# Forty step durations in a kernel's own order model, set to other values (attention and gated MLP on one core)

## The chip, the cores and the metric

The kernel runs on one core of a Trainium2 chip. The metric is the device time of one execution in microseconds, from three runs of each kernel; beside them stands one profiled execution, with its trace.

## The reference

Eight batches, eight heads, 576 positions, head size 64. Each head has two attentions whose results are added; the result then goes, token by token (4608 tokens of 512), through a gated two-layer product.

```python
q_d = q.reshape(B, H, Sd, 4, D).mean(axis=3)       # k_d and v_d likewise, Sd = 144
out_d = softmax_attention(q_d, k_d, v_d)           # all 144 x 144
out_up = np.repeat(out_d, 4, axis=2)
mask = np.abs(pos[:, None] - pos[None, :]) < 4     # a band of 7 around the diagonal
out_local = softmax_attention(q, k, v, mask)
x = (out_up + out_local)                           # -> 4608 x 512
h = x @ w_in                                       # 512 -> 2048
g = h * np.clip(h + 3.0, 0.0, 6.0) / 6.0
out = g @ w_out                                    # 2048 -> 512
```

## The kernel before, in words

*Work.* The tokens are cut into nine chunks of 512 (n = 0 to 8). For a chunk, x is split into a high and a low part (the lines L875 and the casts through L122 and L120). Then come 16 blocks f. A block of the first product, called gemm1 (L972), is 12 matmuls of 128x128 by 128x512: four depths kk of 128 times three pairs of high and low parts. Its result goes into one of two PSUM banks, h0 and h1. ScalarE takes relu (L978), VectorE the gate (L982, after which the bank is free), ScalarE the high part (L986), VectorE or GpSimd the low part (L990). The second product, gemm2 (L1022), adds three matmuls for each of four quarters m of the 512 tokens into four banks o0 to o3 over all 16 blocks. For f = 0 and f = 15 each quarter is a step of its own; for the blocks between, the four quarters are one step of 12 matmuls. After f = 15 each quarter is evicted (L920 on ScalarE, L922 on VectorE) into one of two buffers of the kind `ob`, and stored in four or five pieces (L926, SyncE's queue). A buffer is free when its store has landed.

*Attention* comes in units (b, hp): batch b, pair of heads hp = 0 to 3. The units of b = 0 and 1 run in single steps before and between the first blocks: rows of q, k turned on TensorE (L318) or VectorE (L301), the sums of four rows of v (L409 on TensorE, L394 on VectorE, L396 and L397 on GpSimd), scores of the averaged part (L446), of the band (L640, L648), transposes (L539, L673), products with v (L620, L691), and the adds into x (L696). The units of b = 2 to 7 run as *bursts*: one step on TensorE in which a new unit's averaged scores (L463) and banded scores (L648) and an older unit's products with v (L691, L608) stand together. A burst takes both gemm1 banks, h0 and h1. They are freed by ScalarE's mean (L623) and four pulls (L120), by VectorE's `mean_too` (L626), and by the two adds (L696). L394 sums v, L346 averages q or k; both stand near the adds in VectorE's queue.

*Order.* The order of all work is made on the host, before the program is built, by a list scheduler inside the kernel (`Plan.emit`). Each step is an `op` with an engine, a duration, what it follows, which buffers it takes, and a due time. `emit` runs its own clock: whenever an engine is free in this clock, it starts there the ready step with the earliest `late` time, which is worked back from due times and durations. The steps are then issued in that order, and on the chip each engine runs its queue strictly in order. For steps that several engines can do, `COST[what]` gives a pair (a, b) per engine and the duration is a + b x size; `PEN` adds to the due time. Which `ob` buffer or PSUM bank a step gets is set by the same clock: the one that came free first there. Two lines carry this:

```python
    return {e: (a + b * size, PEN[what].get(e, 0.0)) for e, (a, b) in COST[what].items()}
    l.sort(key=lambda x: (x[0] - (STAY if e == "PE" and kind and x[2].kind == kind else 0.0), x[1]))
```

So a duration in this table changes no instruction; it changes when `emit` believes an engine or buffer to be free, and with that the order of the queues, the choice of engine for steps with a choice, and the choice of buffers.

## Time and profile before

| what | value |
|---|---|
| median of 3 runs (lowest, highest) | 921.95 us (921.82, 923.52) |
| the profiled execution, its span | 922.62 us, 920.8 us |
| mean granted TensorE clock | 0.996 |
| busy: TensorE, VectorE, ScalarE, GpSimd | 902.3, 535.9, 436.8, 217.6 us |
| gemm2 (L1022), 1728 matmuls; gemm1 (L972), 1728 | 412.2 us; 407.0 us |

The span is the time from the first to the last instruction. Busy time counts computing instructions alone. In a row of a timeline stand start, duration, engine, line and operation, and in brackets the engine's idle time ahead of it with what ended it.

### The profile page before, as it was taken

The numbers are of one execution on the slowest core, as the hardware profiler recorded it, in microseconds if no ns is written. First come the engines' busy times: TensorE is split into PE (matmuls) and PEld (weight loads), VectorE is DVE, ScalarE is ACT, GpSimd is POOL, SyncE is SP. The second block draws the span as 40 slices with busy tenths as digits, with TensorE's granted clock in tenths as the row PEclk, the third lists the DMA queues.
The fourth block names the chain that finished last, engine by engine and source line by source line (L and its number), as shares of the span: only waits on it lengthen the run. The fifth ranks groups of instructions, "written<-read, shape, count | busy, mean of one in ns | idle before, by whom it ended". The sixth has DMA issues, their size and how long they took to land.

```text
span 920.8 us, 19166 instructions
## 1 busy us (share of the span) xinstructions
PE 902.3 (98%) x7013; PEld 734.4 (80%) x7013; DVE 535.9 (58%) x973; ACT 436.8 (47%) x1442; POOL 217.6 (24%) x295
## 2 busy tenths in 40 slices
PE   7899999999999999999999999999999999999997
PEld 4577777888778888888888888888888888888886
DVE  6898875677675557556745585557654432233222
ACT  4698754745654456345645555445542222222221
POOL 4626512133342233123302250223201000000000
PEclk9899999999999999999999999999999999999999
DMA  6889542556555555545555556445532010001001
GB/s 205 249 272 274 112 119 63 117 121 130 115 134 111 103 103 127 113 95 113 113 120 104 103 116 136 76 100 117 141 63 53 1 46 1 1 1 46 1 1 46
DMA packets 312398, 93.49 MB, mean 102 GB/s; under 512 B 251504, under 2 KB 297712, under 8 KB 312304
## 3 DMA queue, kind: packets, MB, share of 16 engines
q1 hardware_dynamic: 311024, 90.51, 43.6%
q10 hardware_dynamic: 1280, 1.76, 0.6%
q8 instruction: 55, 0.90, 0.4%
q14 instruction: 39, 0.32, 0.1%
HBM read 69.60 MB, written 22.61 MB: 100 GB/s over the span
## 4 chain that ended last, share of the span: by engine, by line
PE 91%; DMA 3%; SPq 3%; DVE 1%; issue 1%; ACT 0%; ACTq 0%; DVEq 0%
PE h L972 42%; PE o L1022 41%; PE a L648 2%; PE h L691 1%; SPq L295 1%; PE h L608 1%; PE a L463 1%; DMA rawp<-in_w_in_dram 1%; DMA arena<-in_k_dram 1%; DMA arena<-in_q_dram 1%; SPq L369 1%; PE a L446 0%; PE a L691 0%; PE a L620 0%; SPq L373 0%
## 5 line engine op out<-in xcount | busy, mean ns | idle before, releaser
L1022 PE MATMUL o<-wp,rounded 128*128 128x512 f32 x1728 | 412.2, 392 | 0.0
L972 PE MATMUL h<-rounded,wp 128*128 128x512 f32 x1728 | 407.0, 391 | 1.5 <-DVE arena L696 0.9
L972 PEld LDWEIGHTS h<-rounded,wp 128*128 128x128 f32 x1728 | 323.7, 188 | 71.1 <-PE o L1022 1.5
L1022 PEld LDWEIGHTS o<-wp,rounded 128*128 128x128 f32 x1728 | 321.7, 188 | 68.5 <-issue 1.0
L978 ACT ACTIVATE arena<-h 128x512 f32<-128x512 f32 x144 | 85.4, 593 | 181.9 <-PE h L972 179.1
L982 DVE SCALAR_TENSOR_TENSOR arena<-arena,h 128x512 f32<-128x512 f32 x144 | 97.9, 680 | 121.9 <-ACT arena L978 121.7
L990 DVE TENSOR_TENSOR rounded<-arena,rounded 128x512 fp32r<-128x512 f32 x115 | 80.9, 703 | 124.2 <-PE o L1022 106.3
L986 ACT CAST rounded<-arena 128x512 fp32r<-128x512 f32 x144 | 88.9, 617 | 115.0 <-DVE arena L982 59.7
L513 ACT ACTIVATE arena<-arena 128x64 f32<-128x64 f32 x240 | 80.2, 336 | 0.2
L301 DVE STREAM_TRANSPOSE arena<-arena 128x576 f32<-128x576 f32 x56 | 42.7, 764 | 33.6 <-DMA arena<-in_k_dram 22.4
L990 POOL TENSOR_TENSOR rounded<-arena,rounded 128x512 fp32r<-128x512 f32 x29 | 39.2, 1351 | 79.1 <-ACT rounded L986 42.4
L530 POOL TENSOR_TENSOR arena<-arena 128x640 f32<-128x640 f32 (+1 forms) x21 | 24.0, 1143 | 142.3 <-DVE arena L523 142.3
L396 POOL TENSOR_TENSOR arena<-arena 32x256 f32<-32x256 f32 (+1 forms) x28 | 21.7, 775 | 127.2 <-DMA arena<-in_v_dram 121.4
L513 ACT ACTIVATION_READ_ACCUMULATOR arena<-arena 128x1 f32 x240 | 45.1, 188 | 0.0
L623 ACT ACTIVATE arena<-h 128x144 f32<-128x144 f32 x24 | 6.9, 290 | 63.9 <-PE h L608 63.9
L575 DVE STREAM_TRANSPOSE arena<-arena 128x384 f32<-128x384 f32 (+1 forms) x48 | 22.2, 468 | 24.4 <-DMA arena<-pd 24.3
L489 ACT ACTIVATE arena<-arena 128x1 f32<-128x1 f32 (+1 forms) x78 | 15.0, 193 | 42.1 <-DVE arena L502 42.0
L394 DVE TENSOR_REDUCE arena<-arena 128x128 f32<-128x512 f32 (+1 forms) x24 | 25.5, 1062 | 11.0 <-PE h L608 10.8
L352 POOL TENSOR_TENSOR arena<-arena 128x144 f32<-128x144 f32 x50 | 29.6, 592 | 3.9
L594 DVE STREAM_TRANSPOSE arena<-arena 128x640 f32<-128x640 f32 x24 | 20.3, 844 | 17.2 <-DMA arena<-pl 17.0
L648 PE MATMUL a<-arena 64*64 64x64 f32 x1160 | 28.7, 224 | 0.0
L397 POOL TENSOR_TENSOR arena<-arena 32x128 f32<-32x128 f32 (+1 forms) x28 | 12.7, 454 | 61.1 <-PE h L608 60.0
(181 smaller groups left out, 789.8 us busy)
## 6 DMA issues: line engine op xcount, KB each, us to landing
rawp<-in_w_in_dram SPq DMA_DIRECT2D x16, 512.0 KB
rawp<-in_w_out_dram SPq DMA_DIRECT2D x16, 512.0 KB
arena<-in_q_dram SPq DMA_DIRECT2D x112, 72.0 KB
arena<-in_k_dram SPq DMA_DIRECT2D x112, 72.0 KB
pl<-arena SPq DMA_DIRECT2D x24, 320.0 KB
arena<-pl SPq DMA_DIRECT2D x96, 80.0 KB
arena<-in_v_dram SPq DMA_DIRECT2D x28, 256.0 KB
out_dram<-arena SPq DMA_DIRECT2D x89, 72.0 KB
```

The source lines that it names most:

```text
L301: nc.vector.transpose(out=qk[kind], in_=qk[kind])
L352: eng.tensor_tensor(t, t, x[:, :, r], op=ALU.add)
L394: eng.tensor_reduce(out=vd, in_=raw.rearrange("p r e -> p e r"), op=ALU.add, axis=AX.X)
L513: nc.scalar.activation(x[:, j], x[:, j], AF.Exp, bias=m[:, j:j + 1], scale=0.125, accum_out=s[:, j:j + 1])
L530: eng.tensor_tensor(x, x, s.unsqueeze(2).broadcast_to(list(x.shape)), op=ALU.mult)
L648: nc.tensor.matmul(st["ps", g][half:half + WIN, jj * D:jj * D + WIN], qk_of("q")[hs, k_first:k_first + WIN], qk_of("k")[hs, k_first:k_firs ...
L972: nc.tensor.matmul(st["ps"], win[f][:, wt, kk * P:(kk + 1) * P], xs[part][:, kk], start=(kk == 0 and i == 0), stop=(kk == NK - 1 and i == ...
L978: nc.scalar.activation(st["t"], st["ps"], AF.Relu, bias=3.0)
L982: nc.vector.scalar_tensor_tensor(out=t, in0=t, scalar=6.0, in1=st["ps"], op0=ALU.min, op1=ALU.mult)
L986: nc.scalar.copy(st["gh"], st["t"])
L990: eng.tensor_tensor(st["gl"], st["t"], st["gh"].bitcast(F32), op=ALU.subtract)
L1022: nc.tensor.matmul(otile[n, m], gt[:, ms], wout[f][:, wt], start=(f == 0 and i == 0), stop=(f == NF - 1 and i == 2),)
```

## The change: forty durations

Only numbers in the order model change, none of the functions that issue instructions. The core of the diff, with the kinds that the text speaks of:

```diff
-        a = op("ACT", 0.2 + cols / 1070, rebias, lds, take=[place], lag=LAGW)
-        c = op("ACT", 0.2 + cols / 1070, low, lds, lag=LAGW)
-        d = op("DVE", 0.2 + cols / 930, bits, [a, c], lock=not by_bank)
+        a = op("ACT", 0.1 + cols / 1090, rebias, lds, take=[place], lag=LAGW)
+        c = op("ACT", 0.1 + cols / 1090, low, lds, lag=LAGW)
+        d = op("DVE", 0.2 + cols / 1100, bits, [a, c], lock=not by_bank)
...
-        cost = 2.4 if len(both) == 2 else 1.35
+        cost = 2.27 if len(both) == 2 else 1.25
...
-                a = early_user(op("PE", 0.22 if i == 2 else 0.88, partial(turn_rows, i), lds[i:i + 1] if i < 2 else lds[2:],
+                a = early_user(op("PE", 0.17 if i == 2 else 0.63, partial(turn_rows, i), lds[i:i + 1] if i < 2 else lds[2:],
...
-                a = turned[kind] = [op("DVE", 0.66, partial(turn, kind), [l])]
+                a = turned[kind] = [op("DVE", 0.72, partial(turn, kind), [l])]
...
-                sums.append(op({"POOL": on("sum4", 1.0)["POOL"]} if direct else on("sum4", 1.0), 0, partial(sum4, g), [l], take=[("vd" + k0, un)], free=[rk]))
+                sums.append(op({"POOL": on("sum4", 1.0)["POOL"]} if direct else on("sum4", 1 + g), 0, partial(sum4, g), [l], take=[("vd" + k0, un)], free=[rk]))
...
-            od = op("ACT", 0.29, mean, [a], free=[bks[0]])
-            od = op("DVE", 0.31, mean_too, [od], free=[bks[1]])
+            od = op("ACT", 0.2, mean, [a], free=[bks[0]])
+            od = op("DVE", 0.24, mean_too, [od], free=[bks[1]])
...
-            adds = [op("DVE", 0.45, partial(add, g), [a, od], free=[bks[g]], dl=due) for g in range(2)]
+            adds = [op("DVE", 0.38, partial(add, g), [a, od], free=[bks[g]], dl=due) for g in range(2)]
...
-    "ev": {"ACT": (0.15, 1 / 1100), "DVE": (0.13, 1 / 960)},
-    "sum4": {"POOL": (1.3, 0.0), "DVE": (1.03, 0.0)},
-    "pool4": {"DVE": (0.75, 0.0), "POOL": (1.65, 0.0)},
+    "ev": {"ACT": (0.06, 1 / 1180), "DVE": (0.09, 1 / 960)},
+    "sum4": {"POOL": (-0.05, 1.3), "DVE": (0.35, 0.7)},
+    "pool4": {"DVE": (0.67, 0.0), "POOL": (1.74, 0.0)},
...
-    "xhi": {"ACT": (0.15, 1 / 1100), "DVE": (0.1, 1 / 960)},
-    "xlo": {"DVE": (0.2, 1 / 960), "POOL": (0.2, 1 / 440)},
+    "xhi": {"ACT": (0.09, 1 / 1190), "DVE": (0.09, 1 / 960)},
+    "xlo": {"DVE": (0.1, 1 / 960), "POOL": (0.2, 1 / 440)},
```

The other rows are of the same kind (softmax steps, transposes, normalisations; the row for `ob` is unchanged). What the new numbers do to the queues follows at four places. In the rows, a name such as `o_7468` is a PSUM tile, `h_` one of gemm1's two banks or a burst's, `wp_` a block of weights; x2, x3 or x12 counts equal instructions in a row.

TensorE, where chunk 5 ends and chunk 6 begins, around the burst of unit (7,2). Before, the burst (its last rows are L648), then the last four quarters of chunk 5 (o_6472 to o_6495), three gemm1 blocks, and only then the first quarters of the next chunk:

```order
1350 L648 MATMUL a_7350<-arena 64x64 x2
1351 L648 MATMUL a_7351<-arena 64x64 x2
1352 L1022 MATMUL o_6472<-wp_1605,rounded 128x512 x3
1353 L1022 MATMUL o_6477<-wp_1605,rounded 128x512 x3
1354 L1022 MATMUL o_6488<-wp_1605,rounded 128x512 x3
1355 L1022 MATMUL o_6495<-wp_1605,rounded 128x512 x3
1356 L972 MATMUL h_7452<-rounded,wp_579 128x512 x12
1357 L972 MATMUL h_7481<-rounded,wp_712 128x512 x12
1358 L972 MATMUL h_7513<-rounded,wp_720 128x512 x12
1359 L1022 MATMUL o_7542<-wp_755,rounded 128x512 x3
1360 L1022 MATMUL o_7547<-wp_755,rounded 128x512 x3
```

Now:

```order
1354 L648 MATMUL a_7411<-arena 64x64 x2
1355 L648 MATMUL a_7412<-arena 64x64 x2
1356 L1022 MATMUL o_7468<-wp_760,rounded 128x512 x3
1357 L1022 MATMUL o_7491<-wp_760,rounded 128x512 x3
1358 L972 MATMUL h_7502<-rounded,wp_718 128x512 x12
1359 L972 MATMUL h_7536<-rounded,wp_821 128x512 x12
1360 L1022 MATMUL o_7568<-wp_760,rounded 128x512 x3
1361 L1022 MATMUL o_7573<-wp_760,rounded 128x512 x3
```

The last quarters of chunk 5 have moved ahead of the burst (they are above these rows), and the first two quarters of chunk 6 stand directly behind it. The same holds at the bursts (4,2), (5,2) and (6,2).

ScalarE at the same burst. Before, the mean (L623), two pulls, an eviction, and so on by turns; both evictions belong to quarters that ran behind the burst:

```order
744 L623 ACTIVATE arena<-h_7348 128x144
745 L120 COPY arena<-h_7348 64x72 x2
746 L920 ACTIVATE arena<-o_6472 128x512
747 L120 COPY arena<-h_7349 64x72
748 L920 ACTIVATE arena<-o_6477 128x512
749 L120 COPY arena<-h_7349 64x72
```

Now:

```order
750 L623 ACTIVATE arena<-h_7409 128x144
751 L120 COPY arena<-h_7409 64x72 x2
752 L120 COPY arena<-h_7410 64x72 x2
753 L920 ACTIVATE arena<-o_6422 128x512
754 L920 ACTIVATE arena<-o_6498 128x512
755 L489 ACTIVATE arena<-arena 128x1
```

The evictions (of the second and third quarter of chunk 5, which ran ahead of the burst) stand behind the mean and all four pulls. The first quarter is evicted by VectorE now, ahead of the burst's own work. The second quarter's eviction has the same `ob` buffer as the first quarter's, and waits for that store; its bank is the one that `o_7491` above needs.

VectorE at two bursts of the chunk n = 1. Before, at the fourth burst, a transpose of k (L301) and L394 stand ahead of the adds (L696):

```order
326 L990 TENSOR_TENSOR rounded<-arena,rounded 128x512
327 L301 STREAM_TRANSPOSE arena<-arena 128x576
328 L502 TENSOR_REDUCE arena<-a_2852 128x1
329 L626 SCALAR_TENSOR_TENSOR arena<-h_2851,arena 128x144
330 L394 TENSOR_REDUCE arena<-arena 128x128
331 L696 TENSOR_TENSOR first<-h_2850,arena 128x288
332 L696 TENSOR_TENSOR first<-h_2851,arena 128x288
```

Now, at the third:

```order
300 L530 TENSOR_TENSOR arena<-arena 128x640
301 L301 STREAM_TRANSPOSE arena<-arena 128x576 x2
302 L626 SCALAR_TENSOR_TENSOR arena<-h_2657,arena 128x144
303 L394 TENSOR_REDUCE arena<-arena 128x128
304 L696 TENSOR_TENSOR first<-h_2656,arena 128x288
305 L696 TENSOR_TENSOR first<-h_2657,arena 128x288
```

The fourth burst has no such transpose directly ahead any more, the third has it now.

TensorE at the first blocks of chunk 0. Before, block 0 (h_645, in four depths of three matmuls each) ran alone, then blocks 1 and 2:

```order
156 L972 MATMUL h_645<-rounded,wp_579 128x512 x6
157 L409 MATMUL a_737<-arena,four 16x128
158 L446 MATMUL a_740<-arena 64x144 x6
159 L972 MATMUL h_645<-rounded,wp_579 128x512 x3
160 L972 MATMUL h_757<-rounded,wp_712 128x512 x12
161 L972 MATMUL h_784<-rounded,wp_720 128x512 x12
```

Now:

```order
152 L972 MATMUL h_669<-rounded,wp_560 128x512 x3
153 L972 MATMUL h_677<-rounded,wp_633 128x512 x3
154 L972 MATMUL h_669<-rounded,wp_560 128x512 x3
155 L972 MATMUL h_677<-rounded,wp_633 128x512 x3
156 L446 MATMUL a_745<-arena 64x144 x6
157 L972 MATMUL h_669<-rounded,wp_560 128x512 x3
158 L972 MATMUL h_677<-rounded,wp_633 128x512 x3
159 L972 MATMUL h_778<-rounded,wp_718 128x512 x12
```

Blocks 0 and 1 go by turns, depth by depth (the first depth of both stands above these rows), and block 2 follows. On SyncE's queue the first load of w_out now stands ahead of the loads of q and k of unit (1,0); on VectorE the transposes of these q and k stand ahead of the last adds of b = 0.

64 lines of the change are left out of this document (32 added, 32 removed).

## The prediction

> **What bounds the kernel now.** I read the page first: busy time, then the chain that ended last, then the costliest groups.
>
> ```profile
> span 920.8 us, 19166 instructions
> PE 902.3 (98%) x7013; PEld 734.4 (80%) x7013; DVE 535.9 (58%) x973; ACT 436.8 (47%) x1442; POOL 217.6 (24%) x295
> PE 91%; DMA 3%; SPq 3%; DVE 1%; issue 1%; ACT 0%; ACTq 0%; DVEq 0%
> L1022 PE MATMUL o<-wp,rounded 128*128 128x512 f32 x1728 | 412.2, 392 | 0.0
> L972 PE MATMUL h<-rounded,wp 128*128 128x512 f32 x1728 | 407.0, 391 | 1.5 <-DVE arena L696 0.9
> ```
>
> TensorE is busy for 902.3 of 920.8 us, and the two big products alone are 412.2 + 407.0 = 819.2 us. The change removes no matmul, so all it can win is TensorE's idle time, or a slow clock, and all it can lose is new idle time. So the second view is the busy time by stretches, third number TensorE's, with the granted clock.
>
> ```profile
> 40.00:50.00 10.00, 8.57 (x112) 6.32 (x111) 8.94 (x22) 8.25 (x16) 4.69 (x6) 0.83 1.03 385
> 80.00:90.00 10.00, 9.10 (x80) 6.90 (x79) 8.48 (x16) 9.48 (x20) 6.32 (x3) 1.00 1.09 300
> 100.00:110.00 10.00, 8.99 (x59) 6.48 (x61) 9.66 (x14) 7.88 (x17) 5.76 (x5) 1.00 0.29 74
> 300.00:400.00 100.00, 100.00 (x832) 82.80 (x831) 62.52 (x117) 51.90 (x207) 25.25 (x38) 1.00 0.54 111
> 800.00:921.00 121.00, 116.06 (x512) 95.74 (x510) 35.51 (x52) 26.85 (x45) 0.00 (x0) 1.00 0.06 18
> ```
>
> From 300 us on TensorE has no idle time at all (100.00 of 100): there a better order can gain nothing, and a worse one can only lose. The end (800:921) keeps its order. What can be won lies in the first 110 us and in a few waits after that, which the list of TensorE's waits names (us in total, times, longest):
>
> ```profile
> PE a L409 <- DMA early<-in_v_dram: 1.7, 1, 1.7
> PE a L446 <- POOL arena L352: 1.2, 1, 1.2
> PE a L691 <- DVE first L696: 1.2, 1, 1.2
> PE a L409 <- DVE arena L696: 1.0, 1, 1.0
> PE a L539 <- DVE arena L505: 0.9, 1, 0.9
> PE h L972 <- DVE arena L696: 0.9, 1, 0.9
> PE h L972 <- DVE first L696: 0.6, 1, 0.6
> ```
>
> Together 7.5 us. Before dense work has begun, a gap also shifts everything behind it only as far as inputs are there, so not all of that can be had.
>
> **The change part by part.** (1) *The last burst of a chunk (unit (b,2), b = 4 to 7; four places).* A burst takes both gemm1 banks, and before it stood ahead of the chunk's last four quarters of gemm2, with three gemm1 blocks behind them. Now it stands behind those quarters, and directly behind it come the first two quarters of the next chunk's gemm2. Each of these needs a bank that an output eviction (L920 or L922) has emptied. What an undisturbed burst looks like is in the timeline, TensorE, VectorE and ScalarE in turn (start, us):
>
> ```profile
> 386.12 0.48 PE L463 MATMUL a<-arena 64*64 64x144 f32 x8
> 387.61 0.76 PE L648 MATMUL a<-arena 64*64 64x64 f32 x36
> 388.29 5.74 PE L1022 MATMUL o<-wp,rounded 128*128 128x512 f32 x24
> 387.69 1.06 DVE L394 TENSOR_REDUCE arena<-arena 128x128 f32<-128x512 f32 x1 [0.71 <-PE h L608]
> 388.70 0.31 DVE L626 SCALAR_TENSOR_TENSOR arena<-h,arena 128x144 f32<-128x144 f32 x1
> 389.59 0.81 DVE L696 TENSOR_TENSOR first<-h,arena 128x288 f32<-128x288 f32 x2
> 387.82 0.29 ACT L623 ACTIVATE arena<-h 128x144 f32<-128x144 f32 x1 [3.92 <-PE h L608]
> 388.01 0.66 ACT L120 COPY arena<-h 64x72 f32<-64x72 f32 x3
> ```
>
> Call the burst's end B (388.29 there). ScalarE starts the mean (L623) at B-0.47 and has done three pulls (L120) at B+0.38; the fourth ends about B+0.55. In the new order the second quarter's eviction (L920) stands behind these pulls, and its output buffer is the one that the first quarter was evicted into, so that it waits for that store too. Durations of evictions and the return of a buffer:
>
> ```profile
> 360.84 3.33 SPq L926 DMA_DIRECT2D out_dram<-arena  x8
> 364.13 0.69 DVE L922 TENSOR_SCALAR arena<-o 128x512 f32<-128x512 f32 x1 [0.37 <-DMA out_dram<-arena]
> 366.86 0.60 ACT L920 ACTIVATE arena<-o 128x512 f32<-128x512 f32 x1 [1.02 <-DMA out_dram<-arena]
> ```
>
> Eight issues are two stores. The first buffer is back 364.13 - 360.84 = 3.3 us after its store began to be issued, the second, issued from about 362.5, after 366.86 - 362.5 = 4.4 us. In the new order the first quarter ends at B - 2.17 (the burst, 386.12 to 388.29 in that trace) - 3 x 0.68 = B-4.2; its eviction of 0.69 ends about B-3.4, the store is issued at B-3.2, and the buffer is back at B+0.1 to B+1.2. The eviction of the second quarter starts at the later of that and B+0.5, takes 0.60, and a semaphore's way to TensorE is about 0.13: B+1.25 to B+1.9. TensorE is there at B+0.68, the first quarter's three matmuls. So it idles 0.57 to 1.25 us at each place, x4 = 2.3 to 5.0; I take 0.75 each, since a store issued alone shares the queue with less than the two above: **+3.0**. Evictions of quarters three and four have 5.44 us of gemm1 ahead of them and stay covered; if the fourth's store came 2 us later than here, they would wait too. The third gemm1 block needs the bank that the add (L696) frees; the two adds are done at 390.40 = B+2.1, the first about B+1.7, and TensorE comes to it at B+1.9 or later.
>
> (2) *Bursts in the first chunk after the start.* Two waits stand there, 0.9 and 0.6 us in the list; the rows of the second, and the pace of dense work:
>
> ```profile
> 206.32 5.60 PE L972 MATMUL h<-rounded,wp 128*128 128x512 f32 x24
> 211.76 2.88 PE L1022 MATMUL o<-wp,rounded 128*128 128x512 f32 x12
> 241.11 3.02 PE L1022 MATMUL o<-wp,rounded 128*128 128x512 f32 x12
> 241.82 0.78 DVE L301 STREAM_TRANSPOSE arena<-arena 128x576 f32<-128x576 f32 x1 [1.90 <-DMA arena<-in_k_dram]
> 244.73 5.73 PE L972 MATMUL h<-rounded,wp 128*128 128x512 f32 x24 [0.60 <-DVE first L696]
> ```
>
> The first two rows start 5.44 us apart: 24 matmuls, so 0.68 for a quarter of gemm2 (three) and 2.72 for a block of 12. The burst before 241.11 had one block of gemm2 as its cover (2.72 us), and VectorE had sat 1.90 us on a load of k ahead of the adds: the bank came at B+3.5. The new order puts that burst elsewhere, but still puts a transpose (L301) ahead of the adds at one burst of this chunk. I take one of the two waits as gone, the other as left: -0.6 to -1.5, **-0.9**. All other bursts now have one block behind them, which covers 2.72 us against the add's B+1.7. Cost taken: nothing, as long as no late load stands ahead of the adds; without that cover, 0.6 to 0.9 each, as in the two rows of the list.
>
> (3) *The start.* The order of TensorE, VectorE and the loads changes in nearly every line up to 60 us.
>
> ```profile
> 23.57 2.06 SPq L169 DMA_DIRECT2D rawp<-in_w_in_dram  x3
> 31.24 5.49 SPq L295 DMA_DIRECT2D arena<-in_k_dram  x4
> 42.75 0.27 PE L691 MATMUL a<-early 64*64 64x57 f32 x2 [1.15 <-DVE first L696]
> 43.91 2.75 PE L972 MATMUL h<-rounded,wp 128*128 128x512 f32 x6
> 54.05 0.45 PE L640 MATMUL a<-maskb,identb 128*128 128x320 bf16 x2
> 57.91 2.98 PE L972 MATMUL h<-rounded,wp 128*128 128x512 f32 x12
> ```
>
> Before, gemm1 blocks 0 to 2 ran one after another and ended at 54.05; block 3 began at 57.91. Now blocks 0 and 1 run interleaved by quarters of the depth as the quarters of x arrive, so 18 of their 24 matmuls are out of the way before the last quarter. Against that, a weight load of about 2 us (three took 2.06 us of issue at 23.57) is issued ahead of q and k of unit (1,0): k, issued from 31.24 to 36.73 before, comes about 2 us later, VectorE turns it ahead of the last add of unit (0,3), and so the last quarter of x comes near 45.2 by my chaining of these rows. Six matmuls are then left (1.36 us), block 2 waits for the gate of block 0 (about 48.2), and block 3 for that of block 1 on a VectorE that is 90% busy: 55 to 57. Against 57.91 that is -0.9 to -2.9; the waits for L352 and the load of v ahead of it (1.2 + 1.7) go or become others just ahead of these bounds. I take **-1.6**, with -4 (the three waits of 1.7, 1.2 and 1.2 gone, and nothing in their place) and +1 (k later than I chain it) as ends.
>
> (4) *From 60 to 150 us* the planner keeps the same pattern, one attention piece beside each gemm pair; the two waits of 0.9 and 1.0 may go or be replaced: **0**, from -1.9 to +1.5.
>
> Sum: +3.0 - 0.9 - 1.6 + 0 = +0.5. The profiled execution took 922.62 us (span 920.8 and 1.8 around it), 0.67 over the median of 921.95. So 921.95 + 0.5, rounded to **922.4**; half of each term's way to its ends, added as independent, is -1.6 and +1.8: 920.8 to 924.2. This kernel's three runs spread over 1.7 us, so I count anything within 0.2% (1.84 us) as the same.
>
> A rule to weigh, rows first. The gap of 1.15 us at 42.75 lies in the stretch with clock 0.83 (40:50), and six matmuls at 43.91 took 2.75 us instead of 1.36; gaps of 0.9 and 1.0 us at 80:90 and 100:110 left the clock at 1.00. The Trainium skill, "TensorE: Matmul & The Clock Gate", Part 1: The HAM clock gate, says that the clock halves after an idle window of about 3.4 us. By that rule the new gaps of about a microsecond in dense work cost their own length alone; the trace's 0.83 in 40:50, where the longest gap was 1.15, agrees with it only if sparse work counts as idle.
>
> **Rivals.** *Slower: VectorE's adds come late behind a load (place: the burst after each chunk boundary, where the new order has a transpose of k or q, L301, right ahead of L394 and L626).* It decides as soon as that load lands later than the burst's end: the wait at 244.73 and its neighbour in the list show what follows, 0.6 to 0.9 us of idle TensorE. Four such places at 0.6 to 0.9 (2.4 to 3.6), on top of boundary waits at their upper 1.25 (5.0): -0.9 - 1.6 + 5.0 + 1.2 for half of the places = +3.7, **925.7**. Against it stands the list of what L301 waited for between 300 and 700 us (us, times):
>
> ```profile
> DMA arena<-in_k_dram: 12.8, 11
> ```
>
> Eleven late loads of over a microsecond on average, in stretches where TensorE had no idle time.
>
> *Slower: the clock dips at the boundary.* If a boundary wait pulled the clock down, six matmuls at 2.75 - 1.36 = 1.4 us of loss each, x4 = 5.6: **928.0**. The stretches 80:90 and 100:110 speak against it.
>
> *Faster: the start pays in full.* Start -4, chunk one -1.5, boundary at its low end 2.3, sum -3.2: **918.8**. For it: 7.5 us of listed waits are nearly all in what was reordered. Against: most of them are replaced by waits for VectorE, 90% busy there.
>
> *The order changes and the time doesn't.* TensorE's work is the same and saturated; where each new wait equals an old one the sum is 0, 921.95. It falls in the likeliest case's band.
>
> **How the numbers follow.** Likeliest (gains at the start and losses at the boundaries nearly cancel, 922.4, with its own range 920.8 to 924.2): 0.42. Late adds or late stores (925.7): 0.25. Clock dips (928.0): 0.06. Start in full (918.8): 0.27. So faster by over 0.2% 0.27, the same 0.42, slower 0.31. The range 918.0 to 927.0 takes in the first, second and fourth case, and leaves out the dip and the far ends of the start.
>
> **What would show it.** In the profile after: four waits of L1022 for ScalarE's L920, 0.6 to 1.2 us each, right after the burst of a chunk's end (step 1). Neither or one wait of L972 for L696 in 200 to 300 us (step 2). gemm1 block 3 starting at 55 to 57, and a stretch with a clock below 1.00 still there in the first 60 us (step 3). Stretches from 300 to 700 a little under 100 of 100, where they were full. I am wrong if the store is back before the pulls end and the eviction is early (boundary waits under 0.3), if the L301 ahead of L394 waits for its load longer than now, or if the start moves by more than 4 us.

## The result: slower by 5.1 us, and the profile after

| | before | after |
|---|---|---|
| median of 5 runs (lowest, highest), same chip | 921.82 us (920.78, 923.52) | 926.96 us (926.21, 928.87) |
| profiled execution, its span | 922.62 us, 920.8 us | 928.71 us, 926.8 us |
| mean granted TensorE clock | 0.996 | 0.992 |

The ratio is 1.0062, interval 1.0045 to 1.0079: slower. The lines of the page that answer to those of before:

```profile
span 926.8 us, 19232 instructions
PE 905.0 (98%) x7010; PEld 734.6 (79%) x7010; DVE 525.6 (57%) x964; ACT 443.1 (48%) x1452; POOL 216.9 (23%) x303
PE 88%; SPq 5%; DMA 3%; DVE 2%; issue 1%; ACT 1%; ACTq 0%; DVEq 0%
L1022 PE MATMUL o<-wp,rounded 128*128 128x512 f32 x1728 | 416.5, 393 | 2.1 <-ACT arena L920 1.2
L972 PE MATMUL h<-rounded,wp 128*128 128x512 f32 x1728 | 408.7, 392 | 4.7 <-DVE arena L696 2.3
```

VectorE's sum fell by 10 us and the kernel got slower; it is not the bound. In the chain that ended last SyncE's queue (SPq) has 5% where it had 3%, and the idle time ahead of gemm1 rose from 1.5 to 4.7 us. The busy time by stretches (the third number is TensorE's, then come its weight loads, the other engines, the granted clock and the DMA) says where:

```profile
40.00:50.00 10.00, 8.63 (x83) 6.28 (x81) 9.43 (x22) 6.84 (x19) 5.82 (x9) 1.00 1.03 373
60.00:70.00 10.00, 8.70 (x69) 6.76 (x70) 7.87 (x13) 7.65 (x11) 3.67 (x2) 0.83 1.09 322
250.00:300.00 50.00, 46.92 (x486) 38.00 (x479) 33.71 (x69) 24.68 (x101) 12.95 (x20) 0.97 0.59 124
300.00:400.00 100.00, 99.69 (x827) 82.20 (x826) 61.41 (x118) 52.89 (x211) 24.28 (x39) 1.00 0.54 109
```

The same stretch from 250 us of the kernel before:

```profile
250.00:300.00 50.00, 49.13 (x412) 40.47 (x411) 32.92 (x60) 25.23 (x104) 17.57 (x23) 1.00 0.58 122
```

One stretch of 50 us lost 2.2 us of TensorE's time and its full clock. From 300 us on, 0.3 us is missing in each 100. TensorE's waits after (us in total, times, longest):

```profile
PE h L972 <- DVE arena L696: 2.3, 1, 2.3
PE h L972 <- DVE arena L982: 1.2, 1, 1.2
PE o L1022 <- ACT arena L920: 1.2, 4, 0.3
PE h L972 <- DVE first L696: 1.1, 1, 1.1
PE h L463 <- DVE arena L982: 0.8, 1, 0.8
```

To place the whole loss I took the start of each burst in both traces and subtracted TensorE's work issued ahead of it (2.72 us for a block, 0.68 for a quarter, 2.17 for a burst). The difference of the two curves is -1.4 at the first burst, that of unit (2,0). Between the bursts of (3,0) and (3,3) it moves by +1.2, -0.6 and -0.6, together about 0. Then it moves by **+5.3 between the bursts of units (3,3) and (4,0)**, and by +0.53, +0.34, +0.53 and +0.78 at the four chunk ends, **+2.2** together; about -0.1 is left over. Sum +6.0, the difference of the spans (926.8 - 920.8).

**The place of the 5.3.** The changed kernel, around the burst of (3,3): TensorE with the starts of this burst and the one before it, then VectorE, ScalarE and SyncE's queue (start, us).

```profile
270.62 0.48 PE L463 MATMUL a<-arena 64*64 64x144 f32 x8
287.88 0.48 PE L463 MATMUL a<-arena 64*64 64x144 f32 x8
289.24 0.28 PE L463 MATMUL h<-arena 64*64 64x72 f32 x2 [0.77 <-DVE arena L982]
291.18 3.02 PE L1022 MATMUL o<-wp,rounded 128*128 128x512 f32 x12
296.48 7.32 PE L972 MATMUL h<-rounded,wp 128*128 128x512 f32 x24 [2.28 <-DVE arena L696]
...
285.94 0.37 DVE L575 STREAM_TRANSPOSE arena<-arena 32x192 f32<-32x192 f32 x1 [0.97 <-DMA arena<-pd]
290.19 0.78 DVE L301 STREAM_TRANSPOSE arena<-arena 128x576 f32<-128x576 f32 x1 [1.00 <-DMA arena<-in_q_dram]
293.95 0.78 DVE L301 STREAM_TRANSPOSE arena<-arena 128x576 f32<-128x576 f32 x1 [2.40 <-DMA arena<-in_k_dram]
295.89 0.81 DVE L696 TENSOR_TENSOR arena<-h,arena 128x288 f32<-128x288 f32 x2
...
294.11 0.90 ACT L120 COPY arena<-h 64x72 f32<-64x72 f32 x4 [3.10 <-DMA pd<-arena]
...
277.57 3.05 SPq L587 DMA_DIRECT2D arena<-pl  x4
280.71 1.99 SPq L560 DMA_DIRECT2D arena<-pd  x4
282.80 1.83 SPq L565 DMA_DIRECT2D arena<-pd  x4
286.05 2.15 SPq L295 DMA_DIRECT2D arena<-in_q_dram  x4
288.25 2.12 SPq L295 DMA_DIRECT2D arena<-in_k_dram  x4
290.47 1.26 SPq L552 DMA_DIRECT2D pd<-arena  x2
```

Read it from below. The queue is still issuing the read-backs of unit (3,1) (L587, L560, L565) up to 284.6 and two pieces of v up to 285.95, so the loads of q and k for (4,0) (L295) are issued only from 286.05 to 290.37, across the burst's own start, and the small store L552 behind them at 290.47. k's load lands about 3.6 us after its issue ended, and its transpose runs at 293.95. The adds (L696) stand behind that transpose, and ScalarE's four pulls (L120) behind the store. So two chains reach 294 us together, and the gemm1 bank is free at 296.5. TensorE has one block of gemm2 (291.18) as cover, that is, as work that needs no gemm1 bank, and idles 2.28 us. The 0.77 ahead has the same source: the gate stands on VectorE behind a small transpose (L575, 285.94) that waited for L565. The last part is the clock: 24 matmuls take 7.32 us where they take 5.60 elsewhere, 1.72 more. The idle times in brackets go by modelled ends of matmuls and come out too small, so the sum is better taken from start to start. From the burst to its block are 3.30 us (287.88 to 291.18), where the kernel before has 2.17 (289.32 to 291.49): 1.13 more. From the block to gemm1 are 5.30, where experiment 14 has 2.85 without a wait (291.65 to 294.50): 2.45 more. 1.13 + 2.45 + 1.72 is the 5.3. The clock beside it:

```profile
294.10:297.50 3.40, 1.12 (x6) 0.87 (x6) 3.38 (x7) 0.85 (x4) 2.32 (x5) 1.00 0.80 216
297.50:300.90 3.40, 3.40 (x10) 2.63 (x9) 3.21 (x10) 1.55 (x8) 0.40 (x1) 0.50 0.35 48
```

The same burst in the kernel before, with the one ahead of it, and the load of k:

```profile
255.83 0.48 PE L463 MATMUL a<-arena 64*64 64x144 f32 x8
289.32 0.48 PE L463 MATMUL a<-arena 64*64 64x144 f32 x8
291.49 5.74 PE L1022 MATMUL o<-wp,rounded 128*128 128x512 f32 x24
...
282.20 2.12 SPq L295 DMA_DIRECT2D arena<-in_k_dram  x4
```

Two blocks of cover instead of one, and above all 33.5 us between the two bursts instead of 17.3. A unit's transfers occupy SyncE's queue for about 15 us of issue (16.0 us between these two bursts of the changed kernel). With 33.5 us the queue runs ahead of the need, and k's issue is over 5 us before the burst starts; with 17.3 it is 2.5 us after the start.

**A chunk's end**, the changed kernel, TensorE and ScalarE (the burst ends at 367.84):

```profile
367.84 0.97 PE L1022 MATMUL o<-wp,rounded 128*128 128x512 f32 x3
369.11 0.97 PE L1022 MATMUL o<-wp,rounded 128*128 128x512 f32 x3 [0.31 <-ACT arena L920]
...
367.56 0.88 ACT L120 COPY arena<-h 64x72 f32<-64x72 f32 x4
368.46 1.09 ACT L920 ACTIVATE arena<-o 128x512 f32<-128x512 f32 x2
```

The wait that the prediction named, four times. The second quarter starts 1.27 us after the burst's end.

### The profile page after: what moved, and what is told of

Its sections match the earlier page's. It is cut to its first block, busy times and chain, and to the rows that moved or that the text cites. A ratio compares the mean times of both kernels' runs of the same rounds, so it can differ in the third digit from the quotient of the medians.

```text
span 926.8 us, 19232 instructions
## 1 busy us (share of the span) xinstructions
PE 905.0 (98%) x7010; PEld 734.6 (79%) x7010; DVE 525.6 (57%) x964; ACT 443.1 (48%) x1452; POOL 216.9 (23%) x303
## 4 chain that ended last, share of the span: by engine, by line
PE 88%; SPq 5%; DMA 3%; DVE 2%; issue 1%; ACT 1%; ACTq 0%; DVEq 0%
PE h L972 40%; PE o L1022 40%; PE a L648 1%; PE h L691 1%; SPq L295 1%; PE h L608 1%; PE a L463 1%; SPq L926 1%; DMA arena<-in_k_dram 1%; SPq L369 1%; DMA out_dram<-arena 1%; SPq L565 1%; DMA rows<-in_k_dram 0%; PE a L691 0%; PE o L620 0%
## 5 line engine op out<-in xcount | busy, mean ns | idle before, releaser
L1022 PE MATMUL o<-wp,rounded 128*128 128x512 f32 x1728 | 416.5, 393 | 2.1 <-ACT arena L920 1.2
L972 PE MATMUL h<-rounded,wp 128*128 128x512 f32 x1728 | 408.7, 392 | 4.7 <-DVE arena L696 2.3
L972 PEld LDWEIGHTS h<-rounded,wp 128*128 128x128 f32 x1728 | 323.8, 188 | 75.4 <-issue 5.2
L990 DVE TENSOR_TENSOR rounded<-arena,rounded 128x512 fp32r<-128x512 f32 x109 | 76.7, 704 | 131.6 <-PE o L1022 122.0
L990 POOL TENSOR_TENSOR rounded<-arena,rounded 128x512 fp32r<-128x512 f32 x35 | 46.3, 1322 | 190.8 <-PE o L1022 108.9
L301 DVE STREAM_TRANSPOSE arena<-arena 128x576 f32<-128x576 f32 x56 | 43.1, 771 | 37.9 <-DMA arena<-in_k_dram 24.3
L623 ACT ACTIVATE arena<-h 128x144 f32<-128x144 f32 x24 | 7.0, 291 | 70.8 <-PE h L608 70.8
L396 POOL TENSOR_TENSOR arena<-arena 32x256 f32<-32x256 f32 (+1 forms) x25 | 18.8, 754 | 91.1 <-DMA arena<-in_v_dram 90.8
L394 DVE TENSOR_REDUCE arena<-arena 128x128 f32<-128x512 f32 (+1 forms) x27 | 28.6, 1061 | 12.4 <-PE h L608 11.4
L352 POOL TENSOR_TENSOR arena<-arena 128x144 f32<-128x144 f32 x58 | 33.0, 569 | 4.5
L530 DVE TENSOR_TENSOR arena<-arena 128x432 f32<-128x432 f32 (+1 forms) x45 | 32.8, 729 | 1.5
L875 POOL TENSOR_TENSOR rounded<-arena,rounded 128x256 fp32r<-128x256 f32 (+5 forms) x6 | 8.9, 1489 | 98.7 <-ACT rounded L120 87.2
L648 PE MATMUL a<-arena 64*64 64x64 f32 x1180 | 28.9, 222 | 0.0
L202 POOL TENSOR_TENSOR wp<-early,wp 128x1024 fp32r<-128x1024 f32 (+1 forms) x9 | 20.2, 2241 | 31.7 <-ACT wp L198 31.6
```

Of the source, the lines that this page charges most:

```text
L301: nc.vector.transpose(out=qk[kind], in_=qk[kind])
L352: eng.tensor_tensor(t, t, x[:, :, r], op=ALU.add)
L394: eng.tensor_reduce(out=vd, in_=raw.rearrange("p r e -> p e r"), op=ALU.add, axis=AX.X)
L530: eng.tensor_tensor(x, x, s.unsqueeze(2).broadcast_to(list(x.shape)), op=ALU.mult)
L648: nc.tensor.matmul(st["ps", g][half:half + WIN, jj * D:jj * D + WIN], qk_of("q")[hs, k_first:k_first + WIN], qk_of("k")[hs, k_first:k_firs ...
L972: nc.tensor.matmul(st["ps"], win[f][:, wt, kk * P:(kk + 1) * P], xs[part][:, kk], start=(kk == 0 and i == 0), stop=(kk == NK - 1 and i == ...
```

## The experiments

All times are ratios to the kernel before, run on one chip with it. Unless said otherwise the kernels are the changed kernel with single steps moved in the finished order, by the number of the step; no duration is touched, and the other queues stay. The first six ask whether some one queue's order at (3,3) made the loss.

**1. The place undone on SyncE and VectorE.**

```diff
  SyncE, at the burst of (3,3)
+ L552 store of the scores        (then:)
  L295 q of (4,0), L295 k of (4,0)
- L552 store of the scores
  L579 store of the band
  VectorE
- L301 q, L301 k, L346, L626, L664, L696, L696
+ L626, L664, L696, L696, L301 q, L301 k, L346
+ the gate L982 five steps earlier
```

> The changed kernel with its order altered at one place alone, the burst of unit (3,3): on SyncE the store of the averaged weights (L552) stands ahead of the loads of q and k of unit (4,0) again; on VectorE the transposes of these q and k (L301) and the average of q (L346) stand behind the adds (L696), and the gate of block 5 (L982) ahead of the softmax normalisation. Theory A (most of the loss sits at this one place: a wait of 0.77 and one of 2.28 us and a slow clock right behind them, 5.3 us on the curve of lost time between the bursts at 288 and 317 us): 926.96 - 5.3 = 921.7, between 921.2 and 922.7, no wait of L972 above 0.3 us between 280 and 310 us, clock 1.00 there. Rival B (the loss is spread over the new order, or the wait moves on to the next burst because q and k come later): 925 or more, with a new wait at or before the burst near 317.

Ratio 1.0074 (1.0047 to 1.0101): nothing came back. TensorE and VectorE of this kernel:

```profile
293.83 7.39 PE L972 MATMUL h<-rounded,wp 128*128 128x512 f32 x24 [5.18 <-DVE arena L696]
...
292.83 0.49 DVE L664 TENSOR_TENSOR arena<-a,mask 128x320 f32<-128x320 f32 x1 [6.10 <-DMA pl<-arena]
```

L664 stands ahead of the adds and waits for a buffer that the store L579 empties. That store still stands behind the two loads, and is issued only at 289.84. The wait became longer, 5.18. The theory that a load in the wrong order was the cause failed in this form: with L552 ahead, the adds wait for the store that is left behind the loads.

**2. VectorE alone**: the transposes and L346 behind the adds (the VectorE lines of the diff of 1, without the gate).

> The changed kernel with VectorE's queue alone altered at that place: transposes of q and k of unit (4,0) and the average of q behind the adds; SyncE's queue as in the changed kernel. Theory A1 (two things hold the banks: VectorE behind the load of k until 296.3, and ScalarE's pulls, which wait for the store L552 until 294.1 and end at 295.0): L972 starts at about 294.7 to 295.2 instead of 296.48, so a gain of 1.3 to 1.8, up to 3.5 if the slow clock behind it goes too: 923.5 to 925.7. Rival A2 (VectorE's queue alone is the cause): the whole 4.5 us come back, 922.4 or less. Rival B (other places): 926 or more.

1.0054 (1.0035 to 1.0073); of its nine runs one took 3164.56 us, the others 924.71 to 928.66. TensorE and ScalarE:

```profile
292.78 5.69 PE L972 MATMUL h<-rounded,wp 128*128 128x512 f32 x24 [2.28 <-DVE arena L696]
...
290.23 0.90 ACT L120 COPY arena<-h 64x72 f32<-64x72 f32 x4 [2.92 <-DMA pd<-arena]
```

The same 2.28, now through the pulls and the store alone: the adds' own transposes are one of two chains of equal length. The clock did not fall in this execution (24 matmuls in 5.69), so the dip is no fixed part of the wait; why is taken up below.

**3. One number of the forty set back.** A duration of a ScalarE step of 128x10 numbers:

```diff
-            a = op("ACT", 0.12, lambda: nc.scalar.activation(st["m"], ...), [a])
+            a = op("ACT", 0.2, lambda: nc.scalar.activation(st["m"], ...), [a])
```

> The changed kernel with one of the forty durations put back: the 0.12 us of the small ScalarE step that negates the band's maximum is 0.2 us again. By the order, this leaves the first 150 us and the four chunk ends as in the changed kernel, but the burst of unit (3,3) no longer has the loads of q and k ahead of the store on SyncE. Theory A (the place is an accident of the list scheduler, which any small number can make or undo): most of the 5.3 us goes, 921.5 to 924.0, with the four waits at the chunk ends still there. Rival C (the table as a whole makes orders with less slack, one bad place is replaced by another): 925.5 to 928.

1.0002 (0.9986 to 1.0018): the loss is gone. The two bursts are now 24.8 us apart, k's issue is over (281.03 + 2.40) before the burst starts at 284.22, and gemm1 follows its block of cover without a wait. The waits at the chunk ends stay, 0.30 each. So the 5.3 is no property of the forty numbers taken together: the number for one small step decides it, by the order that the list scheduler makes with it.

**4. The place put into the kernel before.**

```diff
  before.py, at the burst of (3,3)
  SyncE:   + q and k of (4,0) behind the stores L552, L579
  VectorE: + L301 q, L301 k ahead of the adds
  TensorE: + one block of gemm2 as cover instead of two
```

> The kernel before with the bad place built into it at the burst of unit (3,3): the loads of q and k of unit (4,0) behind the stores of the weights on SyncE, their transposes behind the low part of block 5 and so ahead of the adds on VectorE, and one block of gemm2 (2.72 us) instead of two behind the burst on TensorE. Theory A (a late load ahead of the adds, and a cover of one block, make the loss by themselves): a wait of L972 of 2 to 3.5 us near 295, a slow clock behind it, +3 to +5.5: 925 to 927.5. Rival B (the place costs little in another surrounding): within 1 us of before, 921 to 923.

1.0006 (0.9987 to 1.0024): no loss at the place. On SyncE this is not the changed kernel's order, in which the loads stand ahead of both stores; it is that of experiment 6. So the run shows one thing: VectorE's order and the single block do no harm where the loads are not late. With 33.5 us since the previous burst they aren't, k's issue is over at 282.13 and the burst starts at 285.77.

**5. Both stores ahead of the loads**, with the VectorE order of 1 (SyncE: L552, L579, then L295 q, L295 k).

> The changed kernel, altered at the burst of unit (3,3) alone: on SyncE both stores of the weights (L552 and L579) ahead of the loads of q and k of unit (4,0); on VectorE the transposes and the average of q behind the adds, the gate of block 5 earlier. Theory D (the loads, 4.3 us of issue, stand ahead of the stores; the stores hold the buffers that the pulls and the band's subtraction L664 write, and both stand ahead of the adds that free the banks): no wait of L972 above 0.3 us there, clock 1.00, 5 us less than the changed kernel: ratio to before 1.000 to 1.002, 0.998 if the start gains as well. Rival E (another wait takes the place again, as the subtraction's wait for L579 did when L552 alone went ahead): a wait of 2 us or more at this burst, ratio above 1.003.

1.0048 (1.0029 to 1.0066). The wait behind the burst is gone, and one block later stands another:

```profile
304.22 7.30 PE L972 MATMUL h<-rounded,wp 128*128 128x512 f32 x24 [3.25 <-DVE arena L982]
```

The transposes wait 1.71 and 1.41 us for q and k, a gate behind them comes late, and the curve loses 5.1 us at this place as before.

**6. SyncE alone**: both stores ahead of the loads, VectorE as in the changed kernel.

> The changed kernel with SyncE's queue alone altered at that burst: both stores ahead of the loads of q and k, VectorE's queue as in the changed kernel. Theory D: the buffers are free early, but k now lands about 1.5 us later, and VectorE's transpose of k stands ahead of the adds: L972 waits until about 9 us behind the burst's end instead of 5.3, so 3 to 5 us more than the changed kernel, ratio 1.009 to 1.012. Rival F (SyncE's queue is the whole cause): the wait goes, ratio 1.002 or less.

1.0097 (1.0064 to 1.0131), and the wait of L972 for L696 is 4.6: the loads come later, and the adds stand behind their transposes. By order alone the loss can be moved or lengthened; none of 1, 2, 5 and 6 removed it. What they share is the queue's lateness: k's issue ends 2.3 us (in 2) to 6.9 us (in 5 and 6) behind the start of the burst.

**7 and 8. The chunk ends**, on the kernel of 3. In 7 the second quarter's eviction goes between the pulls; in 8 the burst goes two quarters up, ahead of the last two quarters of the chunk.

```diff
  7, ScalarE at each chunk end        8, TensorE at each chunk end
  L623, L120 x2                       (quarters 1, 2 of f = 15)
+ L920                              + burst (b,2)
  L120 x2                             (quarters 3, 4 of f = 15)
- L920                              - burst (b,2)
```

> The kernel with one number put back, and at the four chunk ends the eviction of the second quarter (L920) between ScalarE's second and third pull instead of behind the fourth. If the pulls hold the eviction (the store's buffer is back by then), the loss per chunk end falls from 0.5 to about 0.15 us, 1.4 us in all: ratio 0.998 to 0.999. If the store's way back holds it, nothing changes at TensorE, ratio 1.000, or the pulls come later and the wait moves to L972.

> The kernel with one number put back, and at the four chunk ends the burst two quarters of gemm2 (1.36 us) earlier on TensorE, so that three quarters follow it ahead of the one whose eviction is late. By the chain of the second quarter's eviction (B+1.25 for TensorE, or B+2.1 if the store's way back decides now) against TensorE's arrival at B+2.04 the four losses of 0.5 fall to 0.1 or less: 1.6 to 2.0 us in all, ratio 0.998. Rival: the burst's inputs are not ready 1.36 us earlier, and it waits itself: ratio 1.000 to 1.002.

7: 1.0045 (1.0024 to 1.0067); 8: 1.0114 (1.0083 to 1.0145). Both are worse than 3. In 7 the second quarter is no longer late, but the pulls are, and with them the adds:

```profile
363.18 5.74 PE L972 MATMUL h<-rounded,wp 128*128 128x512 f32 x24 [0.86 <-DVE first L696]
```

0.86 at each end in place of 0.30; by the curve 0.6 worse per end. In 8 the waits for L696 reach 1.8, 1.4 worse per end. That is 2.5 of the 4.0 us by which 7 is slower than 3, and 5.6 of the 10.3 of 8; the rest is not explained (the profiled execution of 8 was 9.8 us slower than that of 3 in the first 150 us, where no step was moved). The order that the scheduler chose at the chunk ends costs 0.5 each, and both neighbours cost more there.

**9. The burst of (3,3) 8.2 us later**, behind three more blocks of 12 matmuls, with its followers.

> The changed kernel with the burst of unit (3,3) 8.2 us later on TensorE: the blocks 6 and 7 of gemm1 and one block of gemm2, which followed it, go ahead of it; SyncE's queue as in the changed kernel. Theory G (nothing is wrong with any one queue; the bursts of units (3,2) and (3,3) stand 17.3 us apart, and SyncE needs about 16 us of issue for one unit, so its loads and stores come late for the burst): with 25 us between them the waits of 0.77 and 2.28 us and the slow clock go, 5 us less than the changed kernel, ratio 1.000 to 1.002. Rival H (the loads and stores are late whatever the distance, because they start from the burst before or wait for each other): a wait of 2 us or more remains, ratio above 1.004.

1.0054 (1.0033 to 1.0076). The 2.28 is gone, as the queue had time. But the next burst, (4,0), now follows 17.3 us behind this one, and there the curve loses 3.9:

```profile
312.00 0.28 PE L463 MATMUL h<-arena 64*64 64x72 f32 x2 [1.52 <-DVE arena L982]
```

VectorE had waited 1.98 us for q's load ahead of that gate, and the clock was halved right behind the gap. The loss moved with the close pair, from one unit to the next.

**10. The loads of q and k for (4,0) left out.**

```diff
-            for e in range(4):
+            for e in range(0 if un == (4, 0) else 4):
```

> The changed kernel without the loads of q and k of unit (4,0): this unit works on what the buffers held before. That takes 4.3 us of issue from SyncE's queue and the wait for k from VectorE's, and leaves every order as it is. Theory G: both stores go out 4.3 us earlier, no wait of L972 above 0.3 us at this burst, ratio 1.000 to 1.002. Rival H: the wait remains, above 1 us (the 0.77 us ahead of the burst, for the gate, can stay under both).

1.0001 (0.9983 to 1.0019). Unit (4,0) then works on what its buffers held before. Without these eight transfers the 2.28 is gone and the time is that of before. The wait for the gate is left (0.94): it hangs on L565, which was issued earlier.

**11 and 12. The table in two parts.** In 11 the numbers of the weights and of the first two batches are new and the rest old; in 12 the other way round.

```diff
  11:
-    "ev": {"ACT": (0.06, 1 / 1180), "DVE": (0.09, 1 / 960)},
+    "ev": {"ACT": (0.15, 1 / 1100), "DVE": (0.13, 1 / 960)},
...
```

> The kernel before with those 23 of the forty lines changed that price the weights and the steps of the first two batches; the bursts and the rows for steps with a choice of engine keep the old numbers. By the order it has the changed kernel's kind of start, no eviction behind the pulls at a chunk's end, and three pairs of bursts closer than 18 us. Theory G with the losses as measured (chunk ends 2.2, the place 5.3, start -1.4): 0 to 1.5 us faster than before, ratio 0.998 to 1.000. Rival I (the table's numbers for the start cost by themselves, or another close pair makes a place like that of unit (3,3)): above 1.002.

> The complement: the old numbers for the weights and the first two batches, the new ones for the bursts and for all steps with a choice of engine. By the order, the four chunk ends are as in the changed kernel, and one pair of bursts stands 13.0 us apart. Losses as measured: chunk ends 2.2, start about 0, the close pair 0 (a pair 13.3 us apart had none in the kernel with one number put back) to 5: ratio 1.002 to 1.004, up to 1.008 with the pair. Rival (the four chunk ends' loss came from the start's lateness): ratio 1.000, no waits of L1022 for L920.

11: 1.0041 (1.002 to 1.0062); 12: 1.012 (1.0098 to 1.0141). Their longest waits, of 11 and of 12:

```profile
218.18 5.69 PE L972 MATMUL h<-rounded,wp 128*128 128x512 f32 x24 [2.00 <-DVE first L696]
```

```profile
182.84 7.74 PE L1022 MATMUL o<-wp,rounded 128*128 128x512 f32 x27 [4.42 <-DVE arena L922]
```

In 11 it stands behind a burst that began 16.0 us after the one before it (194.98 and 210.98); 12 has a late eviction in the first chunk, which costs 6.5 us on the curve and was not foreseen, and the four waits of 0.30 at chunk ends. The parts do not add up to the whole (0.41 + 1.2 against 0.62%): each table makes its own order, with its own accidents.

**13. Issue time added**, on the kernel of 3, which has no loss: ten small loads into a spare buffer ahead of q of (4,0).

```diff
+            for e in range(10 if (un, kind) == ((4, 0), "q") else 0):
+                nc.sync.dma_start(spare[:, 8 * e:8 * e + 8], ...)
```

> The kernel with one number put back (no wait at the burst of unit (3,3), last load of k issued 3.0 us ahead of the burst's end), with ten small extra loads (128 rows of 32 bytes into a spare tile) on SyncE's queue ahead of the load of q of unit (4,0): 4 to 5 us more issue time there, nothing else. Theory G (SyncE's time makes the place): k lands 4 to 5 us later, its transpose holds VectorE ahead of the adds, L972 waits 2 to 4 us at this burst, with a slow clock behind it 1.7 more: ratio 1.003 to 1.007. Rival J (slack of this size is there: the kernel has other work to cover it): no wait above 0.5 us, ratio 1.000 to 1.001.

1.0071 (1.0042 to 1.01), against 1.0002 without them. SyncE and TensorE of this kernel (its lines stand three further down: L975 is gemm1, L699 the add, L294 the spare loads):

```profile
281.21 4.88 SPq L294 DMA_DIRECT2D spare<-in_q_dram  x10
...
297.56 2.76 PE L975 MATMUL h<-rounded,wp 128*128 128x512 f32 x8 [3.43 <-DVE arena L699]
```

4.88 us of issue, 40 KB in all, no other order on a compute engine: and the loss is there, 5.8 us on the curve at this place. k's issue ends 2.8 us behind the burst's start (288.46), where in 3 it ended 0.8 ahead of it.

**14. Issue time removed**, from the changed kernel with its 17 us pair: six transfers of unit (3,1) that stand ahead of the loads (two of v, 1.2 us of issue, and the four of L565, 1.83).

```diff
-            for h in range(2):
+            for h in range(0 if un == (3, 1) else 2):
...
-            nc.sync.dma_start(
+            (nothing if (un, h) == ((3, 1), 1) else nc.sync.dma_start)(
```

> The changed kernel without six transfers of unit (3,1) (the four small ones of L565, a part of the averaged weights, and the two of the second half of v), which stood on SyncE's queue right ahead of the loads of q and k of unit (4,0); unit (3,1) then works in part on what the buffers held before. That is 3.1 us less issue time (1.83 + 1.24), with q and k still loaded and every order as it is. Theory G: k and both stores come 3.1 us earlier, the wait of 2.28 us falls to 0.3 or less, the slow clock goes: ratio 1.000 to 1.002. Rival K (what the loads wait for is a buffer or their own landing, not their place in the queue): the wait stays above 1.5 us, ratio 1.005.

1.0009 (0.999 to 1.0027). q and k are still loaded, in the same place of the queue, and VectorE's order is that of the changed kernel. SyncE, and TensorE (gemm2 is L1025, gemm1 L975 here):

```profile
286.30 2.13 SPq L295 DMA_DIRECT2D arena<-in_k_dram  x4
...
291.65 3.02 PE L1025 MATMUL o<-wp,rounded 128*128 128x512 f32 x12
294.50 5.60 PE L975 MATMUL h<-rounded,wp 128*128 128x512 f32 x24
```

k's issue ends 1.0 us before the burst's start (289.47) instead of 2.5 behind it, and gemm1 follows the one block without a wait and at full clock; the curve loses nothing here. 10, 13 and 14 together show the cause: SyncE's issue time, which makes q, k and the stores behind them late for the burst.

Close bursts are how this comes about, but closeness alone does not tell. In the kernel before, with about 15.3 us of issue in 16.9 (to the burst of (3,2)) 0.86 us was lost, with 13.1 in 16.2 (to (3,1)) 0.60, and with 13.9 in 16.0 (to (2,3)) nothing. What tells more is when k's issue ends. At every wait of gemm1 for the adds of over 0.25 us from 150 us on, in all 17 traces, that was behind the burst's start, except at the chunk ends that 7 and 8 alter. It is not enough for a wait: at (2,3) of the kernel before it was 1.3 us behind.

**15. The two waits of the kernel before**, at (3,1) and (3,2): the transposes moved behind the adds there.

```diff
  before.py, VectorE
- L301 k, L502, L626, L394, L696, L696
+ L502, L626, L394, L696, L696, L301 k
...
- L301, L346, L626, L301, L696, L696
+ L626, L696, L696, L301, L346, L301
```

> The kernel before with VectorE's queue alone altered at two bursts, units (3,1) and (3,2): the transposes (L301) and averages of the next unit's q and k behind the adds. Theory G: at these two, both stores stand ahead of the loads on SyncE and only the transposes hold the adds; the waits of 0.60 and 0.86 us go, 1.3 to 1.5 us faster than before, ratio 0.998 to 0.999. Rival L (as at unit (3,3) of the changed kernel, another wait takes their place): ratio 1.000 or more.

1.0002 (0.9986 to 1.0017). The wait of 0.86 went, but at (3,1) there are 0.96 where there were 0.60, and at (3,2) a new one of 0.43 for a gate. No gain that can be measured; no version here beats the kernel before.

## Why the prediction was wrong, point by point

*The likeliest case* (922.4, no change) did not come; 926.96 lies at the upper end of the range, and the change is clearly a loss.

*Step 1, the chunk ends: right in place, mechanism and sign, too large in size.* Forecast +3.0 (0.75 each), measured +2.2 (0.53, 0.34, 0.53, 0.78). Of the two things that could hold the eviction, pulls and returning buffer, the pulls decide: L920 starts at 368.46, 0.02 us after the last pull, and the second quarter at the burst's end +1.27, the early end of the forecast +1.25 to +1.9. The row shows 0.31, less than the curve's 0.5, since the ends of the three matmuls ahead are modelled.

*Step 2, the first chunk: about 0 instead of -0.9.* Both old waits went (-0.6 each on the curve), but a new one came (+1.2). It is at (3,0), which the order had shown with its transposes ahead of the adds. VectorE and TensorE after:

```profile
227.92 0.78 DVE L301 STREAM_TRANSPOSE arena<-arena 128x576 f32<-128x576 f32 x1 [4.38 <-DMA arena<-in_k_dram]
...
230.34 3.92 PE L972 MATMUL h<-rounded,wp 128*128 128x512 f32 x16 [1.11 <-DVE first L696]
```

This burst began 16.0 us after the previous one. In the kernel before, the bursts with the waits of 0.60 and 0.86 stood 16.2 and 16.9 us behind theirs: the waits that the prediction quoted stood at close pairs already, though another pair 16.0 us apart had none. One of the prediction's own signs of being wrong is in these rows: L301 waited 4.38 us for its load, where it had waited 1.90. And there were two waits of L972 for L696 between 200 and 300 us, where it expected at most one.

*Step 3, the start: as forecast in the profile.* Block 3 was to begin at 55 to 57 instead of 57.91:

```profile
55.91 2.98 PE L972 MATMUL h<-rounded,wp 128*128 128x512 f32 x12
```

That is -2.0 there and -1.4 at the first burst, against -1.6. The stretch with the clock at 0.83 did not stay in 40:50; it is in 60:70 now. But the size of this gain can't be taken from one pair of executions: in kernels with the same order up to there the first burst starts at 151.7 to 157.3, once 162.0 (order after), and at 152.5 to 155.4 (order before). So the agreement of -1.4 with -1.6 is partly luck. That something was won is seen in the medians: 3 and 14 keep the four chunk ends (+2.1) and come out 0.2 and 0.8 us above before, so that by estimate 1 to 2 us were won ahead of them, with 1.6 us of uncertainty in each.

*The step that failed* is the sentence "All other bursts now have one block behind them, which covers 2.72 us against the add's B+1.7. Cost taken: nothing, as long as no late load stands ahead of the adds; without that cover, 0.6 to 0.9 each." Whether a load is late was left open, and the order on each engine was read one queue at a time. What was not done: adding up SyncE's issue between two bursts (16.0 us) and holding it against their distance in TensorE's new order (17.3 us at (3,3), where it had been 33.5). That sum would have pointed to the place from the trace of before and the new order; it would not have given the size, as the pairs of the kernel before show. And the price of 0.6 to 0.9 was that of waits at full clock; this one was two gaps, 0.77 and 2.28 in the rows and 3.6 from start to start, and a slow clock of 1.7.

*The rival* "adds come late behind a load" is what happened, with two errors: it sat at one burst and not at the four behind the chunk boundaries, and it cost 5.3 us instead of 1.2. Its time of 925.7 came near by adding the boundary's upper end. "The clock dips at the boundary" did not happen (gaps of 0.3 there); the dip came elsewhere.

*The clock rule that was weighed.* Gaps in dense work, and the 24 matmuls behind them (5.60 us at full speed): 2.28 and 7.32 us in the changed kernel, 2.28 and 5.69 in experiment 2, 5.18 and 7.39 in 1, 3.25 and 7.30 in 5; gaps of about a microsecond left the clock alone, as forecast. The Trainium skill, "TensorE: Matmul & The Clock Gate", Part 1: The HAM clock gate, puts the threshold at an idle window of about 3.4 us that runs free of the kernel. The traces agree with the free-running window: up to the end of the work every halved stretch lasts 3.41 us or a whole multiple of it, and where a trace has several, their starts lie whole multiples apart. They do not agree with a window that has to be idle throughout, and here the measurement decides. In the changed kernel the gap fell whole into one window, 2.28 of 3.41 us idle, and the next window ran at half clock (the two rows at 294.10). In experiment 2 the border of two windows cut the same gap:

```profile
290.90:294.30 3.40, 1.52 (x7) 1.31 (x8) 2.83 (x7) 0.22 (x2) 0.00 (x0) 1.00 0.74 193
294.30:297.70 3.40, 3.40 (x17) 2.81 (x16) 3.25 (x7) 0.00 (x0) 2.73 (x5) 1.00 0.30 42
```

That left 1.9 us idle in one window, and the clock stayed. Between 150 and 850 us of all 17 traces, each window with 1.96 us idle or more was followed by one at half clock, and none with 1.65 or less. Of the six in between one was, with 1.73, in experiment 9, where small matmuls of a burst filled most of the rest. Half a clock for 3.41 us costs 1.7 us.

*What stays open:* how much the start gained, the unexplained part of 7 and 8, and why some late loads of k make a wait and others don't.

## What to carry to other kernels

Where queues run in order, a burst needs its transfers issued, not only its engines free: add up the issue time on the DMA queue between two successive users and compare it with their distance. Where it comes near, as with 16 of 17 us here, look at when the last load is issued: the place is suspect, whatever the engines' shares say, and only a run gives the size. Moving one step in one queue moved the wait here; less issue removed it, and so did the order of experiment 3, with more distance. And a new set of model numbers for a list scheduler is a new draw of the order: one small number made and unmade 5 us here, so judge such a change by several orders, not by one.

## What the hardware showed that was not expected

Small transfers held the issuing queue too: a load of q or k in four pieces held it for 2.0 to 3.4 us around this burst, and ten loads of 4 KB each for 4.88, about 0.49 each. The first 150 us of this kernel scattered by 5 us and more between executions of the same order, so that a gain at the start of that size needs more than one profile. And a gap of TensorE did not need to fill a clock window: 1.96 of 3.41 us was enough to halve the next one, so that the same gap costs 1.7 us more or nothing more, by where the window's border falls.
